# One load queue in program order, other engines issuing the stores, and matmul operands at equal addresses modulo 256

## The chip, the core and the metric

The kernel runs on one core of one Trainium2 chip. The metric is the device time of one execution in microseconds (us); less is better. TensorE does the matrix products, VectorE, ScalarE and GpSimd (POOL) the elementwise work; SP only issues transfers between HBM and the on-chip memory.

## What is computed

```python
def _attn_ref(q, k, v):                      # q, k, v: (8, 8, 576, 64), float32
    k_p = k.reshape(B, H, Sp, 8, D).mean(axis=3)          # pooled by 8: 72 keys
    v_p = v.reshape(B, H, Sp, 8, D).mean(axis=3)
    scores = np.matmul(q, k_p.transpose(0, 1, 3, 2)) / np.sqrt(D)
    attn = np.exp(scores - np.max(scores, axis=-1, keepdims=True))
    attn = attn / (np.sum(attn, axis=-1, keepdims=True) + 1e-09)
    return np.matmul(attn, v_p)

x = attn_out.transpose(0, 2, 1, 3).reshape(4608, 512)
# first layer: w_in (512, 2048), w_out (2048, 512), float64 on the device
r = np.maximum(x @ w_in, 0.0)
x = (s * (r * r) + b) @ w_out
# second layer: w_gate, w_val (512, 1536), w_out2 (1536, 512)
gate = 1.0 / (1.0 + np.exp(-(x @ w_gate)))
out = (gate * (x @ w_val)) @ w_out2
```

## The kernel before

Every float32 matrix is split into a high and a low part (`split`, L54: ScalarE copies the high part, another engine subtracts it), and a product is three matmuls: high by low, high by high, low by high. Weights arrive as 64-bit words and are turned into float32 by `convert` (one ScalarE and three VectorE operations). Tokens are cut into nine blocks of 512. Products over pairs of blocks are done by a scheme with seven products in place of eight, which needs sums and differences of weights and operands; these weights are made once, stored to HBM and loaded again.

The first stage is a loop over 176 slots. Slots 0 to 15 (the prologue) do block 0 while the first layer's weights are converted. Four passes of 40 slots follow, one for each pair of blocks. A slot has two half-steps. In the first, `emit_h` makes one tile of hidden values (12 matmuls into `hps`). In the second, `mm_chunk` does the chunk of two slots ago: 6 matmuls where the chunk number is under 24, and 12 from 24 to 39. Chunks 32 to 39 of a pass have, but for two, no `emit_h` beside them. `prep_chunk` subtracts and splits the operands (`sub` at L297, `operand` making gh and gl). One factor of the scheme, b21, is not kept on the chip: it is stored to `b21d` in the chunks 8 to 15 and loaded again by `reload` into a single buffer `gr`, for the chunks 24 to 31.

The attention of later tokens runs inside the loop in units of 256 tokens, 18 in all. An `events` table gives each step of a unit its half-step, counted from the unit's start: scores of the two halves at 0 and 4 (TensorE, then VectorE subtracts the maximum, ScalarE the exponential), `norm` at 2 and 6 (VectorE sums, GpSimd multiplies into `pl` and `pm`), `turn` (TensorE transposes pm) at 6 and 10, `values` at 12 and 13. Scores, transposes and values share two PSUM buffers of the pool `ps_c`. In a pass units start at half-steps 0, 12, 24 and 36. Keys and values of a batch are loaded by `load_kv` 20 and 13 half-steps ahead of the batch's first unit (L645 to L655) and pooled by GpSimd. The second layer's weights are prepared meanwhile (`prep_w2`, nine parts for each of 12 blocks): loaded, converted, combined, split by ScalarE and GpSimd, and stored.

Loads go out on the SP queue. Stores are put on a list, `later`, and `store_later` issues them on SP at the start of the next slot (L153); `put_x` issues those of the first layer's result on SP, and on GpSimd for the last two blocks. Each issue waits in its queue until its buffer is ready or free, and what is behind it waits too. The order of TensorE's instructions is the program's from slot 16 on (`manual_schedule`, L816). The order on the other engines and on SP is chosen at build time by a scheduler that simulates the program, so that a load may be issued far ahead of its place in the text.

The weights `wr` of `mm_chunk` have three buffers. `fetch_s` asks for a chunk's weights when the chunk three before it is done.

The last stage (L859 on) does the second layer: in each of four pairs of blocks, 12 steps with seven products of 6 matmuls (`product`, weights `w7`, operands `xo`) and 12 matmuls of the output (`emit_o`), then 12 more outputs. `fetch_w7` and `fetch_wo` load weights from SP, `gen_x` makes the operands `xo` from loads issued by GpSimd, and the output is stored from SP.

On-chip memory is handed out from two ends. The pools of constants, operands (gp), weights (wi_p, wr_p, w7p, wo2p) and x lie on the left in the order of their making; the attention's pools and `xop` lie on the right and grow from the end. A tile `pad` of 24 words stands among the constants.

Of the kernel before, what the change touches and what calls it, by code (L numbers as in the profile page):

```python
# [8 lines left out]
F32 = mybir.dt.float32  # L9
# [10 lines left out]
def pooled_attention_two_ffn(ctx, tc, q, k, v, v_left, w_in, w_out, s_in, b_in, w_gate, w_val, w_out2, out):  # L20
# [8 lines left out]
    nc = tc.nc  # L29
# [7 lines left out]
    M1 = w_in.shape[0]  # L37
# [11 lines left out]
    ident = const.tile([128, 128], F32, name="ident")  # L49
    s_sb = const.tile([128, 1], F32, name="s_sb")  # L50
    b_sb = const.tile([128, 1], F32, name="b_sb")
    const.tile([128, 24], F32, name="pad")

    def split(hi, lo, src, eng):  # L54

# [4 lines left out]
    NBLK = len(blocks)  # L60
# [39 lines left out]
    wi_p = w1_stack.enter_context(tc.tile_pool(name="wi_p", bufs=3))  # L100
    rawp = w1_stack.enter_context(tc.tile_pool(name="rawp", bufs=3))
    us_p = w1_stack.enter_context(tc.tile_pool(name="us_p", bufs=1))
    gr_p = w1_stack.enter_context(tc.tile_pool(name="gr_p", bufs=1))
    gs_p = w1_stack.enter_context(tc.tile_pool(name="gs_p", bufs=17))
    wr_p = w1_stack.enter_context(tc.tile_pool(name="wr_p", bufs=3))
    at_stack = ExitStack()
# [43 lines left out]
    def store_later():  # L150
        while later:
            dst, t = later.pop(0)
            nc.sync.dma_start(out=dst, in_=t if t.dtype == F32 else t.bitcast(F32))  # L153

    def load_wo(i):
        if i < M1:
# [139 lines left out]
    def sub(o, a, b_):  # L296
        nc.vector.tensor_tensor(out=o, in0=a, in1=b_, op=ALU.subtract)  # L297
# [16 lines left out]
            wo[p, c] = (t[:, 0], t[:, 1])  # L314

    def reload(p, m):
        ops[p, "b21", m] = gr_p.tile([128, 512], F32, tag="gr", name="gr")
        nc.sync.dma_start(out=ops[p, "b21", m], in_=b21d[m])

    def prep_chunk(p, c, part):  # L320
        j, (z, m) = 1 + 2 * p, divmod(c, H1)
        if part == 0:
            if z == 0:
                src = g_t[j, m]
            elif z == 1:
                src = g_t[j, m + H1]
                later.append((b21d[m], src))
            elif z == 4:
                src = g_t.pop((j, m))
            else:  # L330
                src = g_t[j, m]
                sub(src, g_t[j + 1, m + H1 * (z - 2)], src)
            ops[p, c] = [operand(src)]
        elif z == 3:
            t2, b12, b22 = g_t[j, m], g_t[j + 1, m], g_t.pop((j + 1, m + H1))
            ops[p, c].append(operand(b22))
            sub(b12, b22, b12)
            sub(t2, ops.pop((p, "b21", m)), t2)
        elif z == 4:
            ops[p, c].append(operand(g_t.pop((j + 1, m))))  # L340

# [3 lines left out]
    def put_x(j, d, src):  # L345
        eo = cvp.tile([128, 512], F32, tag="cv", name="eo")
        nc.scalar.activation(out=eo, in_=src, func=ACTF.Identity, scale=s_sb, bias=bias[:, d:d + 1])
        (nc.gpsimd if j >= NBLK - 2 else nc.sync).dma_start(out=x2d[j][:, d, :], in_=eo)

    def add(o, a, b_):  # L350
        nc.vector.tensor_tensor(out=o, in0=a, in1=b_, op=ALU.add)
# [288 lines left out]
    def at(pos, fn, *args):  # L640
        events.setdefault(pos, []).append((fn, args))

    starts = [0, 16] + [2 * M1 + 80 * p + x for p in range(NB1) for x in (0, 12, 24, 36)]
    starts = dict(enumerate(starts[:NU - 2], 2))
    for b in range(1, B):  # L645
        p = starts[b * S // UNIT]
# [9 lines left out]
    for u in range(2, NU):  # L656
        p = starts[u] + (2 if u == 2 else 0)
        for t, o in ((0, 0), (1, 4)):
            at(p + o, scores, u, t, 0)
            at(p + o, scores, u, t, 1)  # L660
            at(p + o + 2, norm, u, t)
            at(p + o + 3, left, u, t)
            if t == 0:
                at(p + 6, turn, u, 0, 0)
                at(p + 6, turn, u, 0, 1)
        at(p + 10, turn, u, 1, 0)
        at(p + 10, turn, u, 1, 1)
        at(p + 7, load_q, u + 2)
        at(p + 12, values, u, 0)
        at(p + 13, values, u, 1)  # L670

    def probs(u, t):
        scores(u, t, 0, True)
# [54 lines left out]
    if True:  # L728
# [83 lines left out]
        for slot, (p, x) in enumerate(chunks):  # L812
            i = hidden.get(slot)
            swap = p is not None and x == 4 * H1 + 1
            if slot == M1:
                pe_order.enter_context(tc.manual_schedule(engines={mybir.EngineType.PE}))  # L816
            store_later()
            for fn, args in events.pop(2 * slot, []):
                fn(*args)
# [25 lines left out]
            while asked < len(used) and used[asked - 3][0] <= slot:  # L845
                _, p1, x1 = used[asked]
                fetch_s(p1, x1 - (x1 < 3 * H1))
                asked += 1
            if p is not None and 3 * H1 - 2 <= x < 4 * H1 - 2:
                reload(p, x - 3 * H1 + 2)  # L850
            if i == NS - M1:
                assert not any(y < 2 * len(chunks) for y in events), events
                at_stack.close()
# [76 lines left out]
        def emit_o(p, m, t):  # L930
            t0, n = pairs[p]
            if m == 0:
                acc[p, t] = [ps_a.tile([128, 512], F32, tag="a", name="acc") for _ in range(n // 128)]
            gh, gl = g2.pop((p, m, t))
            w = wo2.pop((p, t, m))
            hi, lo = w[:, 0], w[:, 1]
            for x, a in enumerate(acc[p, t]):
                f = slice(128 * x, 128 * x + 128)
                nc.tensor.matmul(out=a, lhsT=gl[:, f], rhs=hi, start=m == 0, stop=False)  # L939
                nc.tensor.matmul(out=a, lhsT=gh[:, f], rhs=hi, start=False, stop=False)  # L940
                nc.tensor.matmul(out=a, lhsT=gh[:, f], rhs=lo, start=False, stop=m == M2 - 1)  # L941
                if m == M2 - 1:
                    eo = cvp.tile([128, 512], F32, tag="cv", name="eo")
                    if x % 2:
                        nc.vector.tensor_copy(out=eo, in_=a)
                    else:
                        nc.scalar.activation(out=eo, in_=a, func=ACTF.Copy)
                    r0 = t0 + t * n + 128 * x
                    nc.sync.dma_start(out=out[r0:r0 + 128, :], in_=eo)

        def plain(p, m):

# [84 lines left out]
```

## Time and profile before

| | us |
|---|---|
| median of three timed runs | 1874.98 |
| their range | 1872.32 to 1878.09 |
| the profiled execution | 1883.81 |
| its span, first to last instruction | 1882.0 |
| TensorE busy in it | 1744.7 |
| VectorE busy | 1061.8 |
| ScalarE busy | 751.6 |
| GpSimd busy | 428.5 |

Times of the profile count from the start of the span. A matmul's duration in it overlaps the next one's, so that the distance between two starts, not the duration, says what a matmul costs. "Idle before" is time in which the engine stood still, with what ended it.

### The profile page before, as it was taken

To read this page: it belongs to the slowest core of one execution; us is meant where nothing else is said; L and a number is where in the kernel's file an instruction comes from. 1 tells how busy PE (TensorE), PEld (TensorE's weight loads), DVE (VectorE), ACT (ScalarE), POOL (GpSimd) and SP (SyncE) were. 2 spreads that over 40 slices of the span, in tenths; PEclk is the share of its full clock that TensorE was granted. 3 is DMA by queue.
4 is the path that set the end of the run, shared out by engine and by line. 5 is a ranking of instruction groups with operands and counts; after the bars stand their busy time and mean duration, and the time that the engine had idled before them with its cause. 6 is when DMAs were issued, how large, how long until landed. Compare 5 with 4: busy or idle time off the path is not lost.

```text
span 1882.0 us, 22147 instructions
## 1 busy us (share of the span) xinstructions
PE 1744.7 (93%) x7848; PEld 1432.4 (76%) x7848; DVE 1061.8 (56%) x1636; ACT 751.6 (40%) x1331; POOL 428.5 (23%) x447
## 2 busy tenths in 40 slices
PE   4788898997999989998986999999999999999999
PEld 4566777786778777877875888888888888888887
DVE  7999656666577566656375544555445454544111
ACT  2556555555655556446563322222222222222111
POOL 5788515206360343024141000000000000000000
PEclk8798999998999999999997999999999999999999
DMA  7667978868988787778878455755585558554764
GB/s 269 233 214 240 354 263 285 316 214 293 318 286 266 251 310 269 236 233 264 274 263 309 158 183 199 274 193 198 175 282 185 199 190 284 191 181 171 267 221 149
DMA packets 159550, 454.46 MB, mean 241 GB/s; under 512 B 15696, under 2 KB 37200, under 8 KB 159440
## 3 DMA queue, kind: packets, MB, share of 16 engines
q1 hardware_dynamic: 155920, 441.51, 68.4%
q0 software_dynamic: 3520, 11.54, 1.9%
q8 instruction: 63, 1.03, 0.2%
q14 instruction: 47, 0.39, 0.1%
HBM read 371.20 MB, written 81.79 MB: 241 GB/s over the span
## 4 chain that ended last, share of the span: by engine, by line
PE 55%; DMA 3%; DVE 1%; POOL 1%; ACT 0%; issue 0%; SPq 0%; ACTq 0%; POOLq 0%
PE pc L885 5%; PE pc L884 5%; PE pc L883 5%; PE acc L940 5%; PE acc L941 5%; PE acc L939 5%; PE pb L885 4%; PE pb L883 4%; PE pb L884 4%; PE acc L371 2%; PE acc L372 2%; PE acc L373 2%; DMA wr<-s1d 2%; PE hps L270 2%; PE hps L271 2%; PE hps L272 1%
## 5 line engine op out<-in xcount | busy, mean ns | idle before, releaser
L889 DVE TENSOR_TENSOR wk<-pc,wk 128x512 f32<-128x512 f32 x192 | 132.7, 691 | 248.4 <-PE pc L885 246.7
L270 PE MATMUL hps<-xl,wi 128*128 128x512 f32 (+1 forms) x584 | 242.0, 414 | 12.3 <-DVE xl L57 5.9
L271 PE MATMUL hps<-xh,wi 128*128 128x512 f32 (+1 forms) x584 | 235.6, 403 | 0.0
L272 PE MATMUL hps<-xh,wi 128*128 128x512 f32 (+1 forms) x584 | 235.1, 403 | 0.4 <-POOL wi L57 0.4
L371 PE MATMUL acc<-gl,wr 128*128 128x512 f32 x448 | 178.9, 399 | 28.8 <-DMA wr<-s1d 16.7
L900 ACT ACTIVATE g<-pb 128x512 f32<-128x512 f32 x60 | 35.8, 597 | 357.8 <-PE pb L885 357.8
L748 POOL DMA_DIRECT2D cv<-x2d x36 | 19.8, 551 | 693.6 <-DMA out<-eo 632.2
L372 PE MATMUL acc<-gh,wr 128*128 128x512 f32 x448 | 177.1, 395 | 0.0
L373 PE MATMUL acc<-gh,wr 128*128 128x512 f32 x448 | 176.9, 395 | 0.0
L883 PE MATMUL pc<-xo,w 128*128 128x512 f32 x432 | 170.6, 395 | 0.0
L884 PE MATMUL pc<-xo,w 128*128 128x512 f32 x432 | 170.6, 395 | 0.0
L885 PE MATMUL pc<-xo,w 128*128 128x512 f32 x432 | 170.6, 395 | 0.0
L57 DVE TENSOR_TENSOR gl<-gs,gh 128x512 fp32r<-128x512 f32 x160 | 126.7, 794 | 73.5 <-ACT gh L56 70.2
L56 ACT ACTIVATE gh<-gs 128x512 fp32r<-128x512 f32 x160 | 100.3, 629 | 115.3 <-DVE gs L297 59.2
L57 DVE TENSOR_TENSOR gl<-g,gh 128x512 fp32r<-128x512 f32 x140 | 111.2, 794 | 62.2 <-ACT gh L56 57.4
L56 ACT ACTIVATE gh<-g 128x512 fp32r<-128x512 f32 x140 | 87.8, 627 | 145.4 <-DVE g L901 144.7
L270 PEld LDWEIGHTS hps<-xl,wi 128*128 128x128 f32 x584 | 116.5, 199 | 36.5 <-DVE xl L57 6.1
L57 POOL TENSOR_TENSOR raw<-cv,raw 128x512 fp32r<-128x512 f32 (+1 forms) x72 | 98.8, 1381 | 189.1 <-ACT raw L56 188.8
L272 PEld LDWEIGHTS hps<-xh,wi 128*128 128x128 f32 x584 | 116.2, 199 | 25.3 <-POOL wi L57 0.8
L271 PEld LDWEIGHTS hps<-xh,wi 128*128 128x128 f32 x584 | 116.4, 199 | 21.6
L885 PE MATMUL pb<-xo,w 128*128 128x512 f32 x336 | 132.7, 395 | 0.0
L883 PE MATMUL pb<-xo,w 128*128 128x512 f32 x336 | 132.6, 395 | 0.0
(141 smaller groups left out, 3701.9 us busy)
## 6 DMA issues: line engine op xcount, KB each, us to landing
w<-w7d SPq DMA_DIRECT2D x48, 1792.0 KB, 7.6
wi<-w1d SPq DMA_DIRECT2D x128, 512.0 KB, 5.0
wr<-s1d SPq DMA_DIRECT2D x224, 256.0 KB, 4.3
wo<-wo2d SPq DMA_DIRECT2D x108, 512.0 KB, 4.4
raw<-in SPq DMA_DIRECT2D x68, 512.0 KB, 5.0
w7d<-raw SPq DMA_DIRECT2D x36, 512.0 KB, 4.5
w<-w7d SPq DMA_DIRECT2D x12, 1280.0 KB, 6.8
kv<-in SPq DMA_DIRECT2D x24, 512.0 KB, 6.6
```

What stands on the lines that cost most here:

```text
L56: nc.scalar.activation(out=hi, in_=src, func=ACTF.Copy)
L57: eng.tensor_tensor(out=lo, in0=src, in1=hi.bitcast(F32), op=ALU.subtract)
L270: nc.tensor.matmul(out=ps[:, f], lhsT=hi[:, kk], rhs=c[:, kk, f], start=kk == 0, stop=False)
L271: nc.tensor.matmul(out=ps[:, f], lhsT=hi[:, kk], rhs=a[:, kk, f], start=False, stop=False)
L272: nc.tensor.matmul(out=ps[:, f], lhsT=lo[:, kk], rhs=a[:, kk, f], start=False, stop=kk == KD - 1)
L371: nc.tensor.matmul(out=a, lhsT=w[:, 0, f], rhs=gl, start=begin, stop=False, skip_group_check=True)
L372: nc.tensor.matmul(out=a, lhsT=w[:, 0, f], rhs=gh, start=False, stop=False, skip_group_check=True)
L373: nc.tensor.matmul(out=a, lhsT=w[:, 1, f], rhs=gh, start=False, stop=end, skip_group_check=True)
L883: nc.tensor.matmul(out=ps, lhsT=w[:, 0, x, kk], rhs=r[:, 1, kk, :n], start=first and kk == 0, stop=False, skip_group_check=True)
L884: nc.tensor.matmul(out=ps, lhsT=w[:, 0, x, kk], rhs=r[:, 0, kk, :n], start=False, stop=False, skip_group_check=True)
L885: nc.tensor.matmul(out=ps, lhsT=w[:, 1, x, kk], rhs=r[:, 0, kk, :n], start=False, stop=kk == 1, skip_group_check=True)
L889: nc.vector.tensor_tensor(out=o, in0=ps, in1=b_, op=ALU.add)
```

## The change

The padding among the constants grows from 24 to 56 words, which moves all pools of the left side by 128 bytes; those of the right stay. SP follows the program's order from slot 16 on, as TensorE does. The stores of `store_later` go to GpSimd, those of b21 and of `put_x` to ScalarE, which makes what they store, and the output to GpSimd but for the last block. b21 is loaded again eight chunks later, into the three buffers of the tag "g", and subtracted in the chunks 32 to 39, just before its sum is split. Units start 13 half-steps apart; the second turn and both values come one half-step sooner.

```diff
-    const.tile([128, 24], F32, name="pad")
+    const.tile([128, 56], F32, name="pad")
...
-    gr_p = w1_stack.enter_context(tc.tile_pool(name="gr_p", bufs=1))
...
     def store_later():
         while later:
             dst, t = later.pop(0)
-            nc.sync.dma_start(out=dst, in_=t if t.dtype == F32 else t.bitcast(F32))
+            nc.gpsimd.dma_start(out=dst, in_=t if t.dtype == F32 else t.bitcast(F32))
...
     def reload(p, m):
-        ops[p, "b21", m] = gr_p.tile([128, 512], F32, tag="gr", name="gr")
+        ops[p, "b21", m] = gp.tile([128, 512], F32, tag="g", name="g", bufs=3)
         nc.sync.dma_start(out=ops[p, "b21", m], in_=b21d[m])
...
             elif z == 1:
                 src = g_t[j, m + H1]
-                later.append((b21d[m], src))
+                nc.scalar.dma_start(out=b21d[m], in_=src)
             elif z == 4:
                 src = g_t.pop((j, m))
+                sub(src, ops.pop((p, "b21", m)), src)
...
         elif z == 3:
-            t2, b12, b22 = g_t[j, m], g_t[j + 1, m], g_t.pop((j + 1, m + H1))
+            b12, b22 = g_t[j + 1, m], g_t.pop((j + 1, m + H1))
             ops[p, c].append(operand(b22))
             sub(b12, b22, b12)
-            sub(t2, ops.pop((p, "b21", m)), t2)
...
-        (nc.gpsimd if j >= NBLK - 2 else nc.sync).dma_start(out=x2d[j][:, d, :], in_=eo)
+        nc.scalar.dma_start(out=x2d[j][:, d, :], in_=eo)
...
-    starts = [0, 16] + [2 * M1 + 80 * p + x for p in range(NB1) for x in (0, 12, 24, 36)]
+    starts = [0, 16] + [2 * M1 + 80 * p + x for p in range(NB1) for x in (0, 13, 26, 39)]
...
-        at(p + 10, turn, u, 1, 0)
-        at(p + 10, turn, u, 1, 1)
+        at(p + 9, turn, u, 1, 0)
+        at(p + 9, turn, u, 1, 1)
         at(p + 7, load_q, u + 2)
-        at(p + 12, values, u, 0)
-        at(p + 13, values, u, 1)
+        at(p + 11, values, u, 0)
+        at(p + 12, values, u, 1)
...
             if slot == M1:
-                pe_order.enter_context(tc.manual_schedule(engines={mybir.EngineType.PE}))
+                pe_order.enter_context(tc.manual_schedule(engines={mybir.EngineType.PE, mybir.EngineType.SP}))
...
-            if p is not None and 3 * H1 - 2 <= x < 4 * H1 - 2:
-                reload(p, x - 3 * H1 + 2)
+            if p is not None and 4 * H1 - 2 <= x < 5 * H1 - 2:
+                reload(p, x - 4 * H1 + 2)
...
-                    nc.sync.dma_start(out=out[r0:r0 + 128, :], in_=eo)
+                    (nc.sync if p == NPAIR else nc.gpsimd).dma_start(out=out[r0:r0 + 128, :], in_=eo)
```

## Rows read from the trace of the kernel before

**Rows 1.** Stretches: us, busy of each engine (instructions), granted clock, DMA share, GB/s.
```profile
0.00:204.00 204.00, 147.32 (x672) 122.17 (x673) 179.01 (x242) 102.06 (x189) 156.89 (x154) 0.85 0.72 242
204.00:1008.00 804.00, 741.17 (x3479) 615.04 (x3479) 500.63 (x824) 434.34 (x794) 251.75 (x258) 0.96 0.82 277
1046.00:1882.00 836.00, 831.52 (x3600) 675.22 (x3598) 366.19 (x549) 204.90 (x333) 17.52 (x32) 1.00 0.60 207
```

**Rows 2.** TensorE in time order: start, duration, line, out<-in, shape; both stages.
```profile
997.83 0.39 PE L371 MATMUL acc<-gl,wr 128*128 128x512 f32 x1
...
1003.04 0.39 PE L373 MATMUL acc<-gh,wr 128*128 128x512 f32 x1
...
1103.98 0.39 PE L885 MATMUL pb<-xo,w 128*128 128x512 f32 x1
...
1108.41 0.39 PE L939 MATMUL acc<-wo,gl 128*128 128x512 f32 x1
...
1111.14 0.40 PE L883 MATMUL pb<-xo,w 128*128 128x512 f32 x1
```

**Rows 3.** TensorE's waits in sum: us, times, longest us.
```profile
PE tm L608 <- POOL pm L583: 18.4, 6, 6.9
...
PE sps L556 <- DVE e L564: 13.3, 5, 4.6
...
PE sps L556 <- DVE xl L57: 10.7, 7, 2.1
```

**Rows 4.** TensorE behind long waits (in brackets: idle before, what ended it).
```profile
439.60 1.11 PE L608 MATMUL tm<-ident,pm 128*128 128x128 f32 x4 [6.89 <-POOL pm L583]
...
828.41 0.77 PE L371 MATMUL acc<-gl,wr 128*128 128x512 f32 x1 [3.37 <-DMA wr<-s1d]
...
989.88 0.80 PE L371 MATMUL acc<-gl,wr 128*128 128x512 f32 x1 [7.07 <-DVE gl L57]
...
1022.09 0.76 PE L371 MATMUL acc<-gl,wr 128*128 128x512 f32 x1 [13.33 <-DMA wr<-s1d]
```

**Rows 5.** The SP queue in time order near the end of the first stage.
```profile
979.85 0.52 SPq L153 DMA_DIRECT2D w7d<-raw  x1
...
982.54 0.37 SPq L318 DMA_DIRECT2D gr<-b21d  x1
...
999.88 0.57 SPq L874 DMA_DIRECT2D w<-w7d  x1
...
1004.46 0.91 SPq L313 DMA_DIRECT2D wr<-s1d  x2
```

**Rows 6.** GpSimd in time order, two places.
```profile
426.82 8.14 POOL L462 TENSOR_TENSOR kv<-kv 128x512 f32<-128x512 f32 x5 [6.09 <-DMA kv<-in]
...
967.73 12.09 POOL L57 TENSOR_TENSOR raw<-cv,raw 128x512 fp32r<-128x512 f32 x1 [9.94 <-ACT raw L56]
```

**Rows 7.** The SP queue's own waits in sum, as rows 3.
```profile
SPq L153 <- POOL raw L57: 109.9, 50, 11.7
```

**Rows 8.** Groups of the page: line, operation, count | busy, mean ns | idle.
```profile
L883 PE MATMUL pc<-xo,w 128*128 128x512 f32 x432 | 170.6, 395 | 0.0
...
L883 PE MATMUL pb<-xo,w 128*128 128x512 f32 x336 | 132.6, 395 | 0.0
```

**Rows 9.** DMA issues of the page: count, KB each, median us to landing.
```profile
w<-w7d SPq DMA_DIRECT2D x48, 1792.0 KB, 7.6
```

**Rows 10.** VectorE in time order, one of nine alike, 1.36 us apart.
```profile
402.58 0.69 DVE L57 TENSOR_TENSOR gl<-gs,gh 128x512 fp32r<-128x512 f32 x1 [0.67 <-ACT gh L56]
```

**Rows 11.** Line 348: issues by queue, duration ns min/median/max, first and last start.
```profile
L348 SPq DMA_DIRECT2D x2d<-eo x24: 319/382/1142, 300.3 to 846.5; - x24
...
L348 POOL DMA_DIRECT2D x2d<-eo x8: 542/544/717, 925.0 to 1050.8; - x8
```

**Rows 12.** Line 153: the same for one of its stores.
```profile
L153 SPq DMA_DIRECT2D w7d<-raw x60: 513/519/1014, 307.9 to 997.7; - x60
```

**Rows 13.** One stretch, columns as rows 1.
```profile
967.80:979.80 12.00, 12.00 (x55) 9.93 (x54) 10.86 (x19) 8.62 (x16) 12.00 (x2) 1.00 0.19 67
```

## The prediction

> **What bounds the kernel now.** I read the table by stretch first, then the engine's own starts, then its waits, then the queues behind the longest waits. By stretch [rows 1]: from 1046 us on TensorE is busy 831.5 of 836 us at full granted clock, so there the time is the number of matmuls times their spacing and nothing else. From 204 to 1008 us it is busy 741 of 804 us at a mean clock of 0.96: some 60 us of waits, and a clock that falls behind them. Before 204 us it is busy 147 of 204 us, while VectorE is busy 179 and GpSimd 157: there the elementwise engines set the pace.
>
> Next the spacing of successive matmuls of 512 columns, which is what a busy share hides [rows 2]. Nineteen products of the last stage start 4.43 us apart (1103.98 to 1108.41): 0.2332 us each. The twelve of the output that follow take 2.73 us: 0.2275. Twenty-three of the first stage take 5.21 us: 0.2265. All are of one shape and form; only the products are slow. In the allocation of this program the products are also the only such matmuls whose weights (w7, left side, 96 bytes past a multiple of 256) and moving operand (xo, right side, 224 past) differ modulo 256; wi with xh and xl, wr with gh and gl, gh with wo2 are all at 96.
>
> Then the waits [rows 3]: transposes for GpSimd's pm, scores for the buffer that e or xl must leave. The longest single ones [rows 4] are 13.33 us for wr, 7.07 us for a split gl, 6.89 us for pm, 3.37 us for wr. Two of them come out of the SP queue [rows 5]. At 967.73 a GpSimd operation began that took 12.09 us [rows 6]; the store of its result stood in SP until 979.85, the load of gr behind it went out at 982.54, and VectorE and TensorE waited for that until 989.88. At 999.88 the big loads of w7 went out ahead of the last loads of wr (1004.46), for which TensorE waited until 1022.09. Over the kernel SP stood 109.9 us at stores, waiting for GpSimd [rows 7].
>
> **The change part by part.** All sums are against the profiled execution, 1883.8 us with a span of 1882.0. It is slower than all three timed runs (median 1875.0, highest 1878.1), and the 12.09 us operation may belong to it alone; I take the difference from the median.
>
> **Addresses.** The padding grows by 32 words, so everything on the left moves from 96 to 224 and all pairs agree. There are (432 + 336) times 3 = 2304 products [rows 8]. At the mean 0.2270 of the two other spacings in place of 0.2332 they save 2304 x 0.0062 = 14 us, all of it on the path, for TensorE waits for nothing there. Bounds: 0, and 15.7 at 0.2265. I take 14, because the rows differ in nothing else that I can name. [...]
>
> **Loads in program order, end of the first stage.** The last wr loads come ahead of w7. The 13.33 us goes. New: w7 now goes out when the fourth chunk from the end is done. Its landing takes 7.6 us [rows 9] behind about 1 us of wr issues, against three chunks of 36 x 0.2265 = 8.2 us: 0.4 to 2 us of a new wait. Gain 12 (bounds 11 and 13).
>
> **The reload of b21.** It leaves the stage where VectorE is dense, gets three buffers in place of one and no longer stands behind stores: the 7.07 goes. In its new place each chunk (12 matmuls, 2.72 us) gets a third VectorE operation of 0.69; two idle pieces of 0.67 stand there per chunk [rows 10], which cover it. Its buffers are those of the hidden values g, of which only two come in those eight chunks. If the load is late they don't: a wait of the kind just removed, 7 us, once or more. I take -7 for the old place and +3 for the new (0 to +7).
>
> **Loads kept out of the tail of each pass.** The 3.37 us before 828.41 is a wr load that stood among loads and stores moved ahead: -3.4 (0 to -3.4).
>
> **Units 13 apart.** Before, the values of one unit and the scores of the next fall on one half-step and want the same two PSUM buffers. Today's waits there are 10.7 us behind xl and 13.3 behind e [rows 3], 24 together. One half-step between them (6 or 12 matmuls, 1.4 or 2.7 us) covers the shape with one split of 0.69 and its copy; it does not cover VectorE being behind. Gain 17 (bounds 8 and 24).
>
> **The turn one half-step sooner.** For units at even half-steps pm must be ready 1.4 us sooner, at odd ones 2.7. Of 16 units those that wait now [rows 3] (6 waits, 18.4 us, prologue included) pay in full: three passes x 1.4 = 4.2, and I add 2 for units that come into waiting. +6 (0 to 8 x 1.4 + 8 x 2.7 = 33).
>
> **Stores on GpSimd.** 144 stores of the first stage, counted from the loops: 16 of w1d, 56 of s1d, 60 of w7d, 12 of wo2d. GpSimd spends 0.54 to 0.72 on an issue [rows 11]; it shows none with two runs to a partition, and on SP those take 0.52 where single ones take 0.32 to 0.38 [rows 11, 12], so up to twice. Before slot 16 there are 40: 22 to 44 us of work, into 204 - 157 = 47 us of idle [rows 1]. VectorE's load hides most of it; I take +4 (-3, as SP is freed, to +20). After it some 104 stores, 57 to 114 us, lie in 552 us of idle; uncovered are those just ahead of a pm: +2. The 32 output stores of the last stage lie in 818 us of idle: 0. SP's strict order costs nothing there: w7 is asked for when its buffer comes free and lands 7.6 us later [rows 9], against a step of 54 matmuls, 12.3 us, until it is needed.
>
> **Stores on ScalarE.** 32 of b21d and 32 of x2d at 0.32 to 0.38: 23 us in 370 us of idle [rows 1, 11]; four in a row at the end of a pass delay the next splits, +1.5 (0 to +6). What queues behind them is gh, and for gh wait gl and TensorE.
>
> **Later prefetch.** In program order k and v of a batch load 20 and 13 half-steps ahead and not when a buffer comes free, so GpSimd's pooling moves to where the norms of the unit before stand. That is the picture of 426.82 to 439.60 [rows 4, 6]: pm after 8 us of pooling, a 6.89 us wait. In the first pass of the two it is there already; in the next it would be new: +5 (0 to +14).
>
> **Clock.** [...] Fewer waits give some back: -3 (0 to -10).
>
> Sum: -14 - 12 - 7 - 3.4 - 17 - 3 = -56; +3 + 6 + 6 + 1.5 + 5 = +21; together -35. From the median: 1840.
>
> **The rivals.** *The loop gives its gain back:* waits for e and pm only change their names, since VectorE is behind in any order. What stays is 14 + 12 + 3, less 9 for turn and stores: -20, 1855. For it: more of the scores' waits end with e, VectorE's own work, than with xl [rows 3]. Against it: xl is waited for seven times, at the hand-over that the change pulls apart.
>
> *Addresses do nothing:* -35 + 14 = -21, 1854. Against it stand [rows 2].
>
> *More stalls were SP's than I count:* the splits of raw wait for stores to land, and SP's 109.9 us [rows 7] reach TensorE through them. Of the 63 us of waits between 204 and 1008 us [rows 1] I count 27; if 25 of the other 36 are SP's too: -35 - 25 = -60, 1815. Against it: no wait among the long ones but those named ends with a store.
>
> *Slower, GpSimd as the store queue:* it is one queue in order; a store stands ahead of pm, wi's lower half and the pooling. While VectorE ran 10.86 of 12 us, a GpSimd operation stood for the whole 12 [rows 6, 13]. If the 40 early stores each delay TensorE by 1.1 us (+44), and one stands ahead of each of 32 pm (+35), that is +79 in place of my +6 and of the gain of 17 for the units: 1840 + 73 + 17 = 1930; at half that weight 1840 + 33.5 + 17 = 1890. With the units' gain lost it turns the sign 18 us beyond my +6; early on, GpSimd has no idle left once the 40 issues take over 47 us. [...]
>
> **How the numbers follow.** Forecast 0.50 (own range 1824 to 1856); loop gives back 0.19; addresses nothing 0.08; more 0.13; GpSimd 0.10. This kernel tells about 0.3% (5.6 us) from no change: faster is under 1869.4, slower over 1880.6. Faster: 0.49 + 0.16 + 0.06 + 0.13, and 0.01 of the last rival, 0.85. Slower: 0.08, the rest of that rival but 0.01. Same: 0.07, the near edges of all. The range leaves out GpSimd and the far half of "more": 1812 to 1868.
>
> **What would show it.** Right: products 0.227 apart in the last stage, which is then some 14 us shorter between its first and last product; no wait over 3 us for wr near the end of the first stage, the first w7 waited for under 2 us; scores no longer waiting for xl. Wrong: products still 0.233 apart; "tm behind POOL pm" well over 25 us; the first 204 us longer by over 10; chunks of the last eight of a pass waiting for the reload of b21; wi or wr waited for because SP stands at a load of raw or kv.

## The result, and the profile after

The changed kernel took 1852.4 us (median of 4 runs, 1846.4 to 1855.4) against 1873.7 (4 runs, 1869.6 to 1878.1) for the kernel before beside it: a ratio of 0.988 (95% interval 0.985 to 0.992), 21 us less. The forecast was 35 us less, 1840 us, with a range of 1824 to 1856. The profiled executions, 1882.0 and 1853.6 us of span, differ by 28.4.

Three stretches show where that came from: slots 0 to 15, the loop behind them, and the rest. Slots 0 to 15 end with the last start of L421, the loop with the last start of L372. In these rows of the changed kernel stand durations in ns (min/median/max), then the first and last start in us:

```profile
L421 PE MATMUL acc<-gh,wr x64: 387/389/632, 81.4 to 224.4; 128*128 128x512 f32 x64
...
L372 PE MATMUL acc<-gh,wr x448: 388/389/632, 228.8 to 1016.1; 128*128 128x512 f32 x150
```

In the kernel before, the last starts are 203.8 and 1045.4. So the first 16 slots got 20.6 us longer, the loop 49.9 shorter (841.6 to 791.7), and the last stage not shorter but 0.9 longer (836.6 to 837.5). The forecast in the same stretches was +4, -25 and -14. The sum came near by luck: a miss of 25 one way met misses of 17 and 15 the other way.

The waits of TensorE, as in [rows 3], in the changed kernel (us, times, longest):

```profile
PE acc L370 <- DVE gl L57: 19.9, 12, 6.8
...
PE acc L938 <- DMA wo<-wo2d: 8.9, 3, 3.0
PE tm L607 <- POOL pm L582: 8.9, 3, 4.7
...
PE sps L555 <- DVE xl L57: 6.4, 6, 2.1
...
PE sps L555 <- DVE e L563: 0.5, 1, 0.5
```

Against [rows 3], scores behind e went from 13.3 to 0.5, pm from 18.4 to 8.9, xl from 10.7 to 6.4. The wait for gl, now the longest, was 11.9 us in sum and has grown. New is the wait for wo in the last stage. The long waits at the end of the first stage [rows 4], now:

```profile
984.50 0.80 PE L370 MATMUL acc<-gl,wr 128*128 128x512 f32 x1 [6.75 <-DVE gl L57]
998.26 0.66 PE L370 MATMUL acc<-gl,wr 128*128 128x512 f32 x1 [3.56 <-DVE gl L57]
1018.62 0.56 PE L882 MATMUL pb<-xo,w 128*128 128x512 f32 x1 [2.15 <-DMA w<-w7d]
```

The 13.33 for wr is gone, and w7 is waited for 2.15 us. The 12 us GpSimd operation of [rows 6], which I had thought might belong to one execution, is there again:

```profile
949.49 11.80 POOL L57 TENSOR_TENSOR raw<-cv,raw 128x512 fp32r<-128x512 f32 x1 [7.65 <-ACT raw L56]
```

### The profile page after: what moved, and what is told of

It reads as the page before. It is cut to its first block, busy times and chain, and to the rows that moved or that the text cites. A ratio compares the mean times of both kernels' runs of the same rounds, so it can differ in the third digit from the quotient of the medians.

```text
span 1853.6 us, 22031 instructions
## 1 busy us (share of the span) xinstructions
PE 1728.0 (93%) x7848; PEld 1425.2 (77%) x7848; DVE 1085.4 (59%) x1636; ACT 747.6 (40%) x1331; POOL 522.5 (28%) x615
## 4 chain that ended last, share of the span: by engine, by line
PE 44%; DMA 3%; POOL 1%; DVE 1%; issue 1%; ACT 0%; SPq 0%; POOLq 0%
PE pc L884 5%; PE pc L882 5%; PE pc L883 5%; PE acc L938 5%; PE acc L940 5%; PE acc L939 5%; PE pb L882 4%; PE pb L884 4%; PE pb L883 4%; DMA wo<-wo2d 2%; POOL raw L57 1%; DMA w<-w7d 1%; DMA g<-b21d 0%; DMA raw<-in 0%; DVE gs L296 0%
## 5 line engine op out<-in xcount | busy, mean ns | idle before, releaser
L269 PE MATMUL hps<-xl,wi 128*128 128x512 f32 (+1 forms) x584 | 233.4, 400 | 10.9 <-ACT wi L56 7.7
L271 PE MATMUL hps<-xh,wi 128*128 128x512 f32 (+1 forms) x584 | 229.0, 393 | 0.4 <-POOL wi L57 0.4
L270 PE MATMUL hps<-xh,wi 128*128 128x512 f32 (+1 forms) x584 | 229.0, 392 | 0.0
L948 POOL DMA_DIRECT2D out<-eo x32 | 17.3, 543 | 691.0 <-ACT eo L946 685.4
L370 PE MATMUL acc<-gl,wr 128*128 128x512 f32 x448 | 182.5, 407 | 28.7 <-DVE gl L57 19.9
L372 PE MATMUL acc<-gh,wr 128*128 128x512 f32 x448 | 177.2, 396 | 0.0
L884 PE MATMUL pc<-xo,w 128*128 128x512 f32 x432 | 168.1, 389 | 0.0
L883 PE MATMUL pc<-xo,w 128*128 128x512 f32 x432 | 168.1, 389 | 0.0
L882 PE MATMUL pc<-xo,w 128*128 128x512 f32 x432 | 168.0, 389 | 0.0
L882 PE MATMUL pb<-xo,w 128*128 128x512 f32 x336 | 131.4, 391 | 2.1 <-DMA w<-w7d 2.1
L883 PE MATMUL pb<-xo,w 128*128 128x512 f32 x336 | 131.5, 391 | 0.0
L884 PE MATMUL pb<-xo,w 128*128 128x512 f32 x336 | 131.4, 391 | 0.0
L271 PEld LDWEIGHTS hps<-xh,wi 128*128 128x128 f32 x584 | 111.6, 191 | 24.3 <-POOL wi L57 0.8
```

What stands on the lines that cost most here:

```text
L269: nc.tensor.matmul(out=ps[:, f], lhsT=hi[:, kk], rhs=c[:, kk, f], start=kk == 0, stop=False)
L270: nc.tensor.matmul(out=ps[:, f], lhsT=hi[:, kk], rhs=a[:, kk, f], start=False, stop=False)
L271: nc.tensor.matmul(out=ps[:, f], lhsT=lo[:, kk], rhs=a[:, kk, f], start=False, stop=kk == KD - 1)
L370: nc.tensor.matmul(out=a, lhsT=w[:, 0, f], rhs=gl, start=begin, stop=False, skip_group_check=True)
L372: nc.tensor.matmul(out=a, lhsT=w[:, 1, f], rhs=gh, start=False, stop=end, skip_group_check=True)
L882: nc.tensor.matmul(out=ps, lhsT=w[:, 0, x, kk], rhs=r[:, 1, kk, :n], start=first and kk == 0, stop=False, skip_group_check=True)
```

## The experiments

Twelve kernels were run beside the two. The table gives the last start of L421 ("16 slots"), the length of the loop from there to the last start of L372, and what is left of the span ("rest"), all from the profiled execution. Then come the median and the 95% interval of its ratio to the kernel before, run beside it.

| kernel | 16 slots | loop | rest | median | ratio (95%) |
|---|---|---|---|---|---|
| before | 203.8 | 841.6 | 836.6 | 1873.7 | |
| changed | 224.4 | 791.7 | 837.5 | 1852.4 | 0.985 to 0.992 |
| a1, before with equal addresses | 201.4 | 832.9 | 821.2 | 1857.3 | 0.989 to 0.993 |
| a2, changed with addresses undone | 224.6 | 788.4 | 856.3 | 1866.8 | 0.995 to 0.997 |
| a3, w7 behind wo | 223.5 | 785.0 | 824.9 | 1839.1 | 0.979 to 0.983 |
| a4, early stores on SP | 200.2 | 792.7 | 836.8 | 1829.2 | 0.974 to 0.978 |
| b3, units 12 apart | 224.5 | 807.7 | 843.0 | 1873.6 | 0.998 to 1.001 |
| b4, SP planned in the loop | 238.2 | 811.0 | 836.4 | 1890.7 | 1.007 to 1.010 |
| c1, a3 and a4 | 201.0 | 787.3 | 825.3 | 1815.7 | 0.968 to 0.971 |
| c2, c1 with the old reload | 200.3 | 789.1 | 826.3 | 1817.5 | 0.968 to 0.972 |
| d1, c1 with SP planned | 202.4 | 816.3 | 820.8 | 1841.5 | 0.979 to 0.985 |
| d2, c1 with all these stores on SP | 201.2 | 781.3 | 824.8 | 1808.1 | 0.962 to 0.968 |
| d3, seven offsets (one run) | 223.3 | 786.7 | 850.6 | 1862.5 | |
| d4, c1 with the turn later | 205.6 | 785.7 | 825.1 | 1813.6 | 0.964 to 0.970 |

a1 has the first two stretches of the kernel before unchanged. Its 201.4 and 832.9 against 203.8 and 841.6 show how far one execution is from the next: of the loop's 49.9 some 9 may be the profiled execution of before.

### Addresses (a1, a2, d3)

a1 is the kernel before with a tile of 128 bytes put into the pool of xo, so that xo falls to 96 modulo 256, where w7 is:

```diff
+                if i == NS - M1 + 7:
+                    xop.tile([128, 32], F32, tag="pad2", name="pad2")
```

> The kernel before with one edit: the pool of the last stage's moving operands (xo) lies 128 bytes lower, so that they and the weights w7 are at equal addresses modulo 256 while no other operand moves relative to its partner. Theory (the prediction's: the products pay for the 128 bytes): products of the last stage 0.227 us apart instead of 0.233, about 2016 x 6.7 ns = 13.5 us less; the loop and the outputs as before; time about 1874 - 14 = 1860. Rival one (the address means nothing; the closer products of the changed kernel come from the other parts, such as the queue of the stores): products stay at 0.233, time 1874. Rival two (the products get closer, but the phase of outputs between two pairs gives it back, because loads of wo2d come no sooner): products at 0.227, new waits for wo, time 1868 to 1874.

a2 is the changed kernel with the old padding:

```diff
-    const.tile([128, 56], F32, name="pad")
+    const.tile([128, 24], F32, name="pad")
```

> The changed kernel with the address part alone undone (pad of 24 instead of 56). Theory (address and SyncE order are separate: the waits for wo between two pairs come from the order of the loads, not from faster products): products at 0.233, time about 1852 + 14 = 1866, the three waits of some 3.3 us for wo stay. Rival (the products now run ahead of the loads, and slower ones would take the waits away): products at 0.233, the waits gone, time 1852 to 1856.

To see the products apart from the outputs, take the starts of three matmuls: of the first and the last product of the second pair, and of the first product of the third. The kernel before:

```profile
1228.59 0.40 PE L883 MATMUL pb<-xo,w 128*128 128x512 f32 x1
...
1373.22 0.39 PE L885 MATMUL pc<-xo,w 128*128 128x512 f32 x1
...
1411.54 0.40 PE L883 MATMUL pb<-xo,w 128*128 128x512 f32 x1
```

a1:

```profile
1214.31 0.39 PE L885 MATMUL pb<-xo,w 128*128 128x512 f32 x1
...
1355.52 0.39 PE L887 MATMUL pc<-xo,w 128*128 128x512 f32 x1
...
1393.83 0.39 PE L885 MATMUL pb<-xo,w 128*128 128x512 f32 x1
```

The changed kernel:

```profile
1203.10 0.39 PE L882 MATMUL pb<-xo,w 128*128 128x512 f32 x1
...
1344.31 0.39 PE L884 MATMUL pc<-xo,w 128*128 128x512 f32 x1
...
1387.37 0.39 PE L882 MATMUL pb<-xo,w 128*128 128x512 f32 x1
```

The part with the products takes 144.63, 141.21 and 141.21 us: the 3.4 us are the addresses', 504 products at 6.8 ns. The outputs between the two pairs take 38.32, 38.31 and 43.06. So a1 keeps its gain (17.5 us by the medians, 15.4 in the rest of the span). The changed kernel loses some of it behind three pairs: its outputs there take 41.5, 43.1 and 43.1 us, 12.7 more in sum than in the kernel before. a2 gave 14.5 us back by the medians (its profiled execution, at 1871.1, was 4 us slower than its median, so its rest is longer by more). It kept the waits for wo (9.5 us in sum), so these don't come from faster products.

d3 puts gaps of 32 bytes between the seven tiles of xo:

```diff
+                    if x < 6:
+                        xop.tile([128, 8], F32, tag=f"gap{x}", name=f"gap{x}")
```

> The changed kernel with gaps of 32 bytes between the seven tiles of xo, so that moving operand less weights, modulo 256, is 64, 96, 128, 160, 192, 224 and 0 bytes for xo0 to xo6. Nothing else changes. Theory one (only equality counts): the products with xo6 are 0.2267 apart, the other six 0.233. Theory two (the cost grows with the distance, 128 being the worst): 0.233 at 128 and between that and 0.2267 elsewhere. Theory three (only the distance of 128 costs): 0.2267 for all but xo2. The time: theory one 1852 + 12 = 1864, theory two about 1859, theory three 1854.

Mean distance of the starts within a product, from the trace (some 240 distances for each tile):

| xo less w7, modulo 256 | 0 | 64 | 96 | 128 | 160 | 192 | 224 |
|---|---|---|---|---|---|---|---|
| ns | 226.5 | 232.2 | 234.7 | 231.0 | 233.4 | 231.4 | 232.1 |

Of these seven only equality is free, and the cost has no order by distance, as theory one has it. The distance alone doesn't fix the cost either: in the kernel before, all seven are at 128, and the mean distance of the starts is 234.2 ns for six of them and 232.8 for one, where it is 231.0 here. Why unequal addresses cost what they do stays open. A product at distance 160 beside one at 0, each of 6 matmuls:

```profile
1029.21 0.39 PE L886 MATMUL pc<-xo,w 128*128 128x512 f32 x1
...
1030.61 0.39 PE L886 MATMUL pc<-xo,w 128*128 128x512 f32 x1
...
1031.97 0.40 PE L886 MATMUL pb<-xo,w 128*128 128x512 f32 x1
```

They take 1.40 and 1.36 us. The place of xo relative to the weights matters by itself: a1, which moves nothing but xo, takes 3.4 us off a pair's products.

### The outputs between two pairs (a3)

The SP queue of the changed kernel behind its first pair, and the TensorE wait that it ends in:

```profile
1178.33 3.05 SPq L877 DMA_DIRECT2D wo<-wo2d  x2
1181.72 0.52 SPq L873 DMA_DIRECT2D w<-w7d  x1
1183.78 8.48 SPq L877 DMA_DIRECT2D wo<-wo2d  x4
```

```profile
1194.79 0.50 PE L938 MATMUL acc<-wo,sl 128*128 128x512 f32 x1 [2.88 <-DMA wo<-wo2d]
```

The wo load issued at 1183.78, behind 1.8 MB of w7, landed at 1194.74, 10.96 us later. In the kernel before the same w7 load had gone out at 1190.69, ahead of the outputs, with four rows of wo already asked for.

```diff
-                if m == 4:
+                if m == 8:
                     fetch_w7(p, M2 + 1)
```

> The changed kernel with one number changed: between two pairs the load of the next 1.8 MB of w7d is asked for after output row 8 instead of row 4, that is behind the last of the wo loads. Theory (program order on SyncE puts 1.8 MB between wo loads, and the ones behind it land 8 to 11 us after their issue): no wait for wo, the stretch from the first product of a pair to that of the next falls from 184.4 us to about 180, three times, time about 1852 - 13 = 1839. Rival one (the wo loads are late because of the stores of out and the loads of x2d on the software queue, not w7d): the waits stay, time 1852. Rival two (the load of w7d is now late for its own product, which comes some 20 us after the new place): a new wait for w of several us in each pair, time 1850 to 1865.

1839.1, 13.3 less than the changed kernel. The last product of the second pair and the first of the third:

```profile
1333.56 0.39 PE L884 MATMUL pc<-xo,w 128*128 128x512 f32 x1
...
1371.86 0.39 PE L882 MATMUL pb<-xo,w 128*128 128x512 f32 x1
```

38.30 in place of 43.06, and no new wait for w7 between two pairs. The rival that the output's stores and the loads of x2d held wo up fell with it.

A wait here costs more than itself. Behind the second one, of 3.00 us, the granted clock of the changed kernel fell, to 0.50 from 1378 to 1380 us (columns as in rows 1):

```profile
1377.00:1381.00 4.00, 3.38 (x9) 2.70 (x10) 3.27 (x6) 1.15 (x2) 0.00 (x0) 0.57 0.63 251
```

There six matmuls start 417 to 427 ns apart in place of 227, which makes 1.2 of that pair's 4.75 us. Behind the third wait, of 3.01 us, it fell in the same way (0.57 from 1561.3 to 1565.3 us); behind the first, of 2.88 us, it stayed at 1.00 (1194.2 to 1198.2 us), and that pair loses 3.2 us.

### The first sixteen slots (a4, c1)

VectorE in the changed kernel, one operation, and GpSimd beside it:

```profile
100.25 5.10 DVE L86 TENSOR_SCALAR raw<-raw 128x512 int32<-128x512 int32 x1
```

```profile
99.82 1.10 POOL L184 TENSOR_TENSOR gs<-gs 128x256 f32<-128x256 f32 x1
100.89 1.26 POOL L57 TENSOR_TENSOR wi<-cv,wi 128x512 fp32r<-128x512 f32 x1
102.12 1.26 POOL L461 TENSOR_TENSOR kv<-kv 128x512 f32<-128x512 f32 x1
103.35 1.26 POOL L57 TENSOR_TENSOR wr<-gs,wr 128x512 fp32r<-128x512 f32 x1
104.56 0.57 POOL L152 DMA_DIRECT2D w1d<-wi  x1
```

A VectorE operation whose median is 0.43 us stood for 5.10 while GpSimd ran without a gap. The kernel before has no VectorE operation over 2 us ahead of 260 us; the changed one has 16.

```diff
+    later, early = [], [True]
...
-            nc.gpsimd.dma_start(out=dst, in_=t if t.dtype == F32 else t.bitcast(F32))
+            (nc.sync if early else nc.gpsimd).dma_start(out=dst, in_=t if t.dtype == F32 else t.bitcast(F32))
...
             if slot == M1:
+                early.clear()
```

> The changed kernel with the stores of the first 16 slots (w1d and s1d, those until the manual order begins) back on SyncE; all later stores stay on GpSimd. Theory (the stores that GpSimd issues hold VectorE up: before the change no VectorE operation until 260 us took over 2 us, after it 16 did, up to 5.1 us): these long operations go, the last first-stage chunk ends near 204 to 208 us instead of 224.8, time about 1852 - 18 = 1834. Rival one (the prologue is longer because GpSimd's own queue is longer, and its conversions come later; VectorE's long operations come from GpSimd's arithmetic beside it): long operations stay, gain under 8 us, time 1845 or more. Rival two (SyncE with stores again delays the raw loads): 224.8 stays, time 1852.

1829.2, 23.2 less; the first stretch is back at 200.2. The same line of VectorE (ns min/median/max) in the kernel before, the changed one and a4:

```profile
L86 DVE TENSOR_SCALAR raw<-raw x68: 376/430/1523, 19.9 to 1003.8; 128x512 int32<-128x512 int32 x68
```

```profile
L86 DVE TENSOR_SCALAR raw<-raw x68: 376/429/5101, 19.5 to 978.9; 128x512 int32<-128x512 int32 x68
```

```profile
L86 DVE TENSOR_SCALAR raw<-raw x68: 378/429/1519, 18.8 to 958.2; 128x512 int32<-128x512 int32 x68
```

With the 40 stores of these slots off GpSimd the long operations are gone ahead of 190 us. VectorE's busy time in the first stretch was 178.8 us before, 189.9 in the changed kernel and 178.0 in a4, and what TensorE waits there for gl (L420 before, L419 in the others) 1.7, 16.0 and 3.1.

An issue need not be there for VectorE to stand. In d1 (below) GpSimd only computes from 208.20 to 213.81 us, and a VectorE operation that took 0.69 us at 203.18 starts at 209.04 and ends at 214.37:

```profile
209.04 5.33 DVE L57 TENSOR_TENSOR raw<-gs,raw 128x512 fp32r<-128x512 f32 x1
```

```profile
208.03 1.47 POOL L184 TENSOR_TENSOR wsum<-wsum,gs 128x512 f32<-128x512 f32 x1
209.25 0.92 POOL L184 TENSOR_TENSOR gs<-gs 128x256 f32<-128x256 f32 x1
209.93 3.88 POOL L461 TENSOR_TENSOR kv<-kv 128x512 f32<-128x512 f32 x3
```

So VectorE stood beside GpSimd's arithmetic alone. Whether the 40 issues closed GpSimd's gaps, or the planner (the scheduler at build time) laid out the first slots in another order for them, these runs don't tell. Nor do they show why VectorE stands; in the changed kernel it did so from 100.25 to 105.35 us, through four instructions of GpSimd, the issue among them.

c1 has both edits, that of a3 and that of a4.

> The changed kernel with both of the edits that took time out singly: the load of w7d behind the wo loads (-13.3 us alone) and the stores of the first 16 slots on SyncE (-23.2 us alone). Theory (the two lie in different stages and add up): 1852 - 13 - 23 = 1816. Rival (a later wait takes one of them): 1822 to 1830.

1815.7, and 1852.4 less 13.3 and 23.2 is 1815.9: they add up.

### Units and turn (b3, d4)

```diff
-    starts = [0, 16] + [2 * M1 + 80 * p + x for p in range(NB1) for x in (0, 13, 26, 39)]
+    starts = [0, 16] + [2 * M1 + 80 * p + x for p in range(NB1) for x in (0, 12, 24, 36)]
```

> The changed kernel with the attention units 12 half-steps apart again instead of 13; the earlier turns and values stay. Theory (the prediction's term: units 13 apart take some 17 us of waits out of the first four passes): the passes z = 0 to 2 of each p grow by 8 to 24 us in all, time 1852 + 17 = 1869 (1860 to 1876). Rival (the passes are shorter because of the earlier turns and because SyncE no longer carries stores, and the distance of the units does nothing): time 1849 to 1856.

1873.6, 21 us more; in the profiled execution 16.0 more in the loop and 5.5 in the rest, where the units have no part. The wait at the hand-over, 6.4 us in the changed kernel, came back:

```profile
PE sps L555 <- DVE xl L57: 19.1, 13, 2.6
```

d4 is c1 with a later turn of the second half:

```diff
-        at(p + 9, turn, u, 1, 0)
-        at(p + 9, turn, u, 1, 1)
+        at(p + 10, turn, u, 1, 0)
+        at(p + 10, turn, u, 1, 1)
```

> As c1, with the turn of a unit's second half back one half-step later (10 instead of 9) and the values where the changed kernel has them (11 and 12). Theory (the prediction's term: the earlier turn adds 6 us of waits for pm, and more for lt): time 1815 - 6 = 1809, waits of tm and tl smaller. Rival (with the turn later the values come one half-step behind it, and wait for VectorE's t instead): 1815 to 1830.

1813.6 (1811.1 to 1819.2) against 1815.7 (1814.9 to 1821.5): no difference that their spread allows. No cost of the earlier turn shows.

### The reload of b21 (c2)

c2 is c1 with the old place of the reload. Beside the lines shown it has the padding of 24 words and xo moved as in a1, so that the operands stay at equal addresses.

```diff
+    gr_p = w1_stack.enter_context(tc.tile_pool(name="gr_p", bufs=1))
-            if p is not None and 4 * H1 - 2 <= x < 5 * H1 - 2:
+            if p is not None and 3 * H1 - 2 <= x < 4 * H1 - 2:
...
-                sub(src, ops.pop((p, "b21", m)), src)
...
+            sub(t2, ops.pop((p, "b21", m)), t2)
```

> As c1, with the reload of b21 and its subtraction back where the kernel before had them (a buffer of its own, one pass earlier, subtracted on VectorE within the fourth pass); the last stage's operands are kept at equal addresses by moving the pool of xo. Theory (the new place costs the last eight chunks of each p some 5 us, which wait for the reload that is asked for only two chunks ahead): the fifth passes fall from about 31 us to 25.5, 1816 - 12 = 1804. Rival (the old place costs VectorE as much in the fourth pass and at the turn, the 7 us that the prediction gave for it): 1812 to 1820.

1817.5, the same as c1. VectorE's subtraction in c1, where it reads g, and in c2, where it reads gr (count | busy, mean ns | idle before, what ended it):

```profile
L296 DVE TENSOR_TENSOR gs<-g,gs 128x512 f32<-128x512 f32 x96 | 75.6, 817 | 57.5 <-ACT g L277 28.7 <-DMA g<-b21d 28.7
```

```profile
L297 DVE TENSOR_TENSOR gs<-gr,gs 128x512 f32<-128x512 f32 x32 | 26.9, 840 | 7.3 <-DMA gr<-b21d 7.3
```

The new place does make VectorE wait, 28.7 us against 7.3, and TensorE waits 18.6 us for gl in c1 and 2.7 in c2. But in c2 TensorE has other waits in their stead: 9.4 us for wr, where c1 has 3.9, and 9.3 for wi, where c1 has none.

```profile
PE acc L371 <- DMA wr<-s1d: 9.4, 9, 2.9
PE hps L270 <- DMA wi<-w1d: 9.3, 4, 4.1
```

### The order of the loads, and who stores (b4, d1, d2)

b4 is the changed kernel with SP left to the planner until the last chunk of the first stage; d1 is c1 with the same edit.

```diff
-                pe_order.enter_context(tc.manual_schedule(engines={mybir.EngineType.PE, mybir.EngineType.SP}))
+                pe_order.enter_context(tc.manual_schedule(engines={mybir.EngineType.PE}))
...
         store_later()
+        pe_order.enter_context(tc.manual_schedule(engines={mybir.EngineType.PE, mybir.EngineType.SP}))
```

> The changed kernel with SyncE ordered by the planner until the last first-stage chunk has been emitted, as in the kernel before, and in program order from there on (the last stage keeps its order). Theory (the prediction's terms: the load queue in program order is what shortened the end of the first stage, by 12 us, and the wr loads in the tails, by 3.4): the last sixteen chunks grow from 74.5 us to 86 or more, time 1852 + 15 = 1867. Rival one (the end of the first stage is shorter because the stores of w7d left SyncE, whoever orders the loads): time 1849 to 1856. Rival two (strict order costs the loop more than it gives, since a load whose buffer is not free holds the ones behind it): time 1835 to 1848.

> As c1, with SyncE ordered by the planner until the last first-stage chunk (the edit of b4, which cost 38 us on the changed kernel, 14 of them before slot 16, where GpSimd carried the stores). Theory (b4's loss in the first stretch needs the stores on GpSimd; the rest is what program order of the loads is worth in the loop): the first 16 slots stay at about 201 us, the loop loses some 20, time 1815 + 22 = 1837. Rival one (program order is worth the whole 38 wherever the stores are): 1853. Rival two (the planner's order was only bad together with early stores on GpSimd): 1813 to 1821.

b4: 38 us more by the medians; in the profiled execution 14 ahead of slot 16 and 19 in the loop. The planner lays out VectorE, ScalarE and GpSimd together with SP, so other queues change with it, and these two runs don't show the order of the loads alone. d1: 26 us more than c1, 29 in the loop. There the picture of [rows 4, 6] is back. A load of values in d1, GpSimd's pooling of it, and TensorE's waits:

```profile
419.54 1.44 SPq L452 DMA_DIRECT2D kv<-in  x2
```

```profile
427.24 6.34 POOL L461 TENSOR_TENSOR kv<-kv 128x512 f32<-128x512 f32 x4 [6.61 <-DMA kv<-in]
433.54 0.74 POOL L582 TENSOR_TENSOR pl<-e,sm 128x64 f32<-128x64 f32 x1
434.24 1.49 POOL L582 TENSOR_TENSOR pm<-e,sm 128x512 f32<-128x512 f32 x1
```

```profile
435.79 1.11 PE L607 MATMUL tm<-ident,pm 128*128 128x128 f32 x4 [5.41 <-POOL pm L582]
...
995.26 0.77 PE L370 MATMUL acc<-gl,wr 128*128 128x512 f32 x1 [5.57 <-DMA wr<-s1d]
```

The planner asks for these values as soon as a buffer is free, and GpSimd pools them ahead of pm. In c1, in program order, those of the same batch (the sixth) go out at 455.22, and the pooling comes behind pm:

```profile
464.77 1.03 POOL L582 TENSOR_TENSOR pm<-e,sm 128x512 f32<-128x512 f32 x1
465.78 4.39 POOL L461 TENSOR_TENSOR kv<-kv 128x512 f32<-128x512 f32 x3
```

From slot 16 on c1 has one idle stretch of TensorE over 1.5 us ahead of the transposes of pm (2.0); d1 has four (7.6, 5.4, 6.8, 4.0). Only two of the four, 9.4 us, end with pm. The 7.6 and the 6.8 end with VectorE's e, behind an operation that stood beside GpSimd as in the first slots: the 5.33 us above, and this one of 9.83 us, through which GpSimd pooled, combined and split without a gap:

```profile
528.54 9.83 DVE L591 TENSOR_TENSOR lt<-pl,lt 128x128 fp32r<-128x128 f32 x1 [1.72 <-ACT lt L590]
```

TensorE's wait at 995.26 is for a wr load that went out at 980.08, behind two loads of w7 (976.75 and 978.50), and landed 15 us later.

d2 is c1 with all stores of `store_later` on SP:

```diff
-            (nc.sync if early else nc.gpsimd).dma_start(out=dst, in_=t if t.dtype == F32 else t.bitcast(F32))
+            nc.sync.dma_start(out=dst, in_=t if t.dtype == F32 else t.bitcast(F32))
```

> As c1, with every store of store_later on SyncE, those of w7d and wo2d in the loop too; loads and stores then go out in one program order. Theory (the loads must not stand behind stores that wait for GpSimd's splits: in the kernel before SyncE stood 109.9 us at them): SyncE stands again for about that long, loads of wi, wr and raw come late, TensorE waits for them, time 1815 + 15 to 40, so 1830 to 1855. Rival (a store waits only for what the chunk before has already made, and nothing of the loads is near its limit): 1811 to 1821.

1808.1 (1805.4 to 1810.3), below c1, the fastest of all and 44 us below the changed kernel. SP stands at the stores as long as ever, as in [rows 7]:

```profile
SPq L152 <- POOL raw L57: 109.2, 28, 12.0
```

In its whole trace no VectorE or GpSimd operation takes over 2 us; the GpSimd operation of 12 us is gone too.

## Why the prediction was right, and where it was not

**The loop in one table.** TensorE's waits between the last starts of L421 and of L372, in us, against what the prediction forecast for their terms:

| TensorE waits for | before | changed | difference | forecast |
|---|---|---|---|---|
| the buffer of the scores (sps, behind e and xl) | 21.4 | 4.3 | -17 | -17 |
| wr | 16.7 | 5.1 | -12 | -15 |
| gl | 11.9 | 19.9 | +8 | -4 |
| the transposes of pm (tm, behind pm and e) | 18.8 | 2.1 | -17 | +13 |

The forecasts are those of the units (-17), of the end of the stage and the tails (-12 - 3.4), of the reload (-7 + 3), and of the turn, the later prefetch and the later stores on GpSimd (+6 + 5 + 2). All waits together went from 76.2 to 39.8 us, 36.3 less of the loop's 49.9. The other part is TensorE's own work: the same matmuls keep it busy 13.6 us less, at a higher granted clock (before, then changed):

```profile
203.80:1045.40 841.60, 765.44 (x3577) 634.68 (x3576) 516.18 (x846) 444.79 (x810) 254.24 (x262) 0.95 0.81 276
```

```profile
224.40:1016.10 791.70, 751.88 (x3578) 621.41 (x3576) 529.62 (x839) 437.89 (x801) 325.22 (x363) 0.98 0.83 286
```

**Addresses, -14: right.** a1 gave 17.5, a2 took 14.5. The rival that they do nothing fell with them. (Its upper bound of 15.7 comes to 15.4 by the spacings it states.)

**"SP's strict order costs nothing there: 0": wrong, +13.** The step asked only whether w7 comes in time for its own product. It did (2.15 us once). It didn't ask what is queued behind it on SP: wo. That ate the addresses' gain (a3).

**Units, -17: right.** The table has it, and undone it cost 21, 16 of them in the loop (b3).

**Stores on GpSimd, +4 in the first slots: mis-sized, 20.6 to 23 measured.** The bound of +20 was close; the choice was wrong. I set the issues against GpSimd's idle time and took VectorE's load as cover. It was the other way round: VectorE is the busiest engine there [rows 1], and it was held up while GpSimd had more to do (VectorE busy for 189.9 us, against 178.0 in a4). What stood was the other side than in the slower rival: there a GpSimd operation for 12 us, here one of VectorE for 5.10. The count of 40 was right for these slots, but the planner let 18 stores of later slots out among them: by 224.4 us 58 had gone out, at medians of 0.59, 0.78 and 1.10 us for the three kinds. Over 10 us more in the first 204 was a sign of being wrong, and it came.

**End of the first stage, -12, and the reload, -7 + 3.** The last sixteen chunks took 87.3 us in a1 and 74.5 in the changed kernel, 12.8 less: the size of the loads' part, with nothing left for the reload's. The cause is wider than I said. With SP planned (d1) they take 73.5, though w7 goes ahead of wr again; with the stores on SP in program order (d2) 70.6; with the old reload (c2) 74.9. So neither the order nor the stores' place nor the reload's is needed by itself; no run undoes two of them. The reload's place is worth nothing in the end (c2): a wait moved. The late chunks waiting for the reload were another sign of being wrong, and came too (28.7 us of VectorE's time in c1). The -3.4 in the tails was not tried apart; no wait for wr in the changed kernel is over 1.3 us.

**The turn, +6: mis-sized, 0** (d4), the low bound.

**"Later prefetch", +5: wrong sign.** The prediction read the 6.89 us wait of [rows 4] as one that would come again in another pass, where it was one that would go. With the turn's +6 it is the largest miss of the loop: the waits ahead of the transposes fell by 17 us and were to rise. The likely cause is where the pooling falls: loads at a fixed distance ahead put it behind pm, and the planner had put it ahead. With SP planned the loop is 19 to 29 us longer (b4, d1). But in d1 9.4 us of these waits end with pm and 14.4 behind standing VectorE operations, and no run moves the loads of keys and values alone, so this cause is argued and not shown.

**The clock, -3 (0 to -10): mis-sized, -13.6**, or -11.0 against a1, where TensorE is busy 762.8 us in the loop. No run shows the 3 us as a term of its own, nor the clock apart from the waits; what the runs show is the loop's granted clock, 0.95 before and 0.98 in the changed kernel, and the busy time above.

**The rivals.** 1852 lies nearest to "addresses do nothing", 1854, and "the loop gives back", 1855, and yet both fell: the loop gave 41 (against a1) to 50 us. SP's 109.9 us at stores [rows 7], the ground of "more stalls", are no cost by themselves: d2 has as many (109.2) and is fastest. Taking the stores of `store_later` off SP brought nothing: putting the early ones back took 23 us off, the others some 8 more.

**Left open.** The stores of b21d and x2d on ScalarE (+1.5) and the output's on GpSimd were not tried apart.

## What to carry to other kernels

Before a queue is put into a fixed order, go through each large load in it and ask what lands late behind it (here wo, after 10.96 us), not only whether it is itself in time. An engine with idle time is no free place for stores where a busier one stands still while it works: look for operations far above their own median (here 5.10 us against 0.43). Count a wait of TensorE with the clock that falls behind it (here 1.2 us behind one of 3.00). Where two stretches of equal matmuls have different spacings (here 233.2 and 226.5 to 227.5 ns), compare the operands' addresses modulo 256.

## What the runs showed of the hardware

- A matmul of 512 columns costs 226.5 ns where weights and moving operand are at equal addresses modulo 256, and 231 to 235 at six other distances (d3, a1).
- A VectorE operation whose median is 0.43 us stood for 5.10 us while GpSimd worked without a gap (the changed kernel); another stood for 5.33 us beside GpSimd arithmetic without an issue in it (d1).
- Behind two of three like waits of 2.9 to 3.0 us TensorE's granted clock fell, to 0.57 over 4 us against 1.00 behind the other, and six matmuls started up to 427 ns apart in place of 227 (the changed kernel).
- GpSimd's issue of a store of w1d, w7d or s1d takes 0.59 to 0.81 us (medians over the changed kernel), SP's of w1d or s1d 0.38 to 0.54 (a4).
- A load of 0.5 MB behind one of 1.8 MB on the same queue landed after 11 us (the changed kernel); the median of wo in the kernel before was 4.4.
